# Two feed-forward layers in split float32: the second layer's first product by seven products of halves

## The chip, the cores and the metric

One core of one Trainium2 chip runs the program. Its engines are TensorE (PE in the rows), VectorE (DVE), ScalarE (ACT), GpSimd (POOL) and the DMA queues, which SyncE (SP) issues. The metric is the device time of one execution in microseconds. The profile is one execution taken by the hardware profiler.

## The reference

Linear attention with a normalised output, then two feed-forward layers. Only the second layer is changed.

```python
kv  = einsum('bhsd,bhse->bhde', k, v)                 # 4 batches, 8 heads, 576 tokens, 64
out = einsum('bhsd,bhde->bhse', q, kv)
x   = out / sqrt(mean(out*out) + 1e-6) * g_norm       # -> [2304 tokens, 512]
h = x @ w_in;  g = max(h, 0) + log1p(exp(-abs(h)));          x = g @ w_out      # first layer
h = x @ w_in2; g = where(h > 0, h, exp(min(h, 0)) - 1);    out = g @ w_out2     # second layer
```

The inner width d_ff is 2048. The weights are float64 in the reference; all results are float32.

## The kernel before

**Operands.** Every operand of the feed-forward products is carried as two parts, hi and lo, whose sum is the float32 value. A product a x b is three matmuls: hi x hi, lo x hi, hi x lo. The weights lie in DRAM as float64 words; `weights` turns a chunk of them into float32 by integer work (DMA L236, ACT L244 and L247, DVE L251, L255, L260 and L264) and splits it (ACT L271, DVE or POOL L275). A chunk has two halves: half 0 for the first product (w_in), half 1 for the second (w_out).

**Tiling.** The 2304 tokens go in 6 blocks of 384. d_ff goes in 16 chunks of 128, and these in 4 quarters. For each layer and quarter all blocks are swept; a block's sum over a quarter's 4 chunks stays in a PSUM bank and is added to `acc_sb` in SBUF at the quarter's end (L606 copies, L612 adds, L621 adds and L624 stores the result). A unit is (layer, quarter, block, chunk); each layer has 96. `unit_h` makes the first product of a unit (L486, 12 matmuls of 384 columns: 4 pieces of d_model x 3). `unit_act` applies the nonlinearity: in layer 1 seven instructions (L507 to L528), in layer 2 three (L507, L534, L537); then ACT casts the hi part (L541) and DVE or POOL makes the low part (L545). `unit_out` makes the second product three units later: in layer 1 four row chunks, in layer 2 three row chunks of 3 matmuls with 512 columns (L579 to L581). `next_x` (L630, L632) splits layer 1's sums into the token operands of layer 2.

**PSUM.** Two banks hold the h of two units, four the sums of the second product, one is used by transposes (`m`), one by attention (`o`).

**What sets the order.** The instructions are written as strands. The class `Order` (L47) lists them greedily: each engine's next instruction is the one with the lowest key among those it could start, by rough costs (`pe`, `act`, `dve`, `pool`, `dma`, L27 to L44), by marks that say what is there and by rings that count buffers. The order of each engine is then fixed in the program; each engine runs its list in turn and waits at an instruction until what it needs is there. `main` (L654) is PE's list of units; a strand of weights has the key of the unit that first needs them, less `W_LEAD`.

Of the kernel before, what the change touches and what calls it, by code (L numbers as in the profile page):

```python
# [25 lines left out]
# Rough costs in ns, for the order of issue alone.  # L26
def pe(n, passes=1):  # L27
    return passes * n / 2.4 + 3
# [18 lines left out]
class Order:  # L47
    """The order of issue: strands of instructions, listed greedily on the engines.

    A strand is a generator. Before each instruction it yields (engines, needs): a tuple of  # L50
    (engine, cost[, bias]) to choose from, and the marks that have to be there; it is sent the engine.
    Of the instructions that an engine could start, the one with the lowest key goes first. The
    data's own waits are the framework's; a poor estimate costs time only.
    """
# [9 lines left out]
    # From then on VectorE has the time, and GpSimd would only take its port from it.  # L64
# [9 lines left out]

    def add(self, key, strand):
        s = [key, strand, None, self.end if self.strands else 0.0]
        self.strands.append(s)
        s[2] = next(strand, None)
        if s[2] is None:
            self.strands.remove(s)  # L80
        return s

# [13 lines left out]
    def when(self, need):  # L96
        """The time a need is met, None if it isn't yet."""
# [20 lines left out]
    def run(self):  # L118
        while self.strands:
# [11 lines left out]
            if not heads:  # L131
                raise RuntimeError("no strand can go on")
# [13 lines left out]
            s[3] = self.end if e != PE else done  # L146
            try:
# [9 lines left out]
def linear_attention_then_two_ffns(  # L157
# [35 lines left out]
    WSLOTS = QF + 3  # L193
# [4 lines left out]
    ps = ctx.enter_context(tc.tile_pool(name="ps", bufs=1, space=bass.MemoryType.PSUM))  # L198

    # PSUM: its banks by use.  # L200
# [27 lines left out]
    w_t = {}  # L228
    convs = []

    def weights(i):
        layer, fc, half = convs[i]
# [8 lines left out]
        # The 29 bits that go, as a count of the last place that stays.  # L241
        yield ((ACT, act(512)),), [ring("r"), ("conv", i - 1)]
        r, r_h = sbuf("r", 1, f"r{n}", dtype=U32)
        nc.scalar.activation(r, low, AF.Copy, scale=2.0**-29)  # L244
        yield ((ACT, act(512)),), [ring("q")]
        q, q_h = sbuf("q", 3, f"q{n}", uses=2)
# [15 lines left out]
        # Below the smallest normal float32: zero.  # L262
# [3 lines left out]
        )  # L266
        drop(c_h)
        mark("conv", i)
        yield ((ACT, act(512)),), [ring(f"whi{half}"), ("split", i - 1)]
        hi, hi_h = sbuf(f"whi{half}", WSLOTS, f"whi{n}", dtype=F32R)  # L270
        nc.scalar.copy(hi, q)  # L271
        drop(q_h)
# [519 lines left out]
```

## Time and profile before

| | |
|---|---|
| time, median of 3 runs | 877.72 us (877.53 to 878.41) |
| span of the profiled execution | 875.8 us |
| PE busy | 860.6 us (98%) |
| DVE busy | 652.1 us (74%) |
| ACT busy | 490.2 us (56%) |
| POOL busy | 72.7 us (8%) |
| DMA, hardware queue | 52.44 MB, 18.3% of 16 engines |

The profiled execution is shown by its span, from the first to the last instruction; the times of the runs are taken around it. Layer 1's first product starts at 19.12 us, layer 2's at 462.13 us (its second unit at 467.92). Start and duration of an instruction come from the trace; matmuls are pipelined, so the distance from one start to the next says more of their cost than the duration of one.

### The profile page before, as it was taken

The numbers are of one execution on the slowest core, as the hardware profiler recorded it, in microseconds if no ns is written. First come the engines' busy times: TensorE is split into PE (matmuls) and PEld (weight loads), VectorE is DVE, ScalarE is ACT, GpSimd is POOL, SyncE is SP. The second block draws the span as 40 slices with busy tenths as digits, with TensorE's granted clock in tenths as the row PEclk, the third lists the DMA queues.
The fourth block names the chain that finished last, engine by engine and source line by source line (L and its number), as shares of the span: only waits on it lengthen the run. The fifth ranks groups of instructions, "written<-read, shape, count | busy, mean of one in ns | idle before, by whom it ended". The sixth has DMA issues, their size and how long they took to land.

```text
span 875.8 us, 12932 instructions
## 1 busy us (share of the span) xinstructions
PE 860.6 (98%) x4954; PEld 812.6 (93%) x4954; DVE 652.1 (74%) x1228; ACT 490.2 (56%) x1033; POOL 72.7 (8%) x62
## 2 busy tenths in 40 slices
PE   7999999999999999999999999999999999999998
PEld 7788899999999999999998999999999999999997
DVE  5899887788898887889999764787458864744543
ACT  4777887777676776667776544553234432322221
POOL 0441110010111000001021000000000000000000
PEclk8999999999999999999999999999999999999999
DMA  9953210201101101010011220122001200000111
GB/s 279 307 171 107 89 61 25 73 28 57 61 26 50 63 33 49 25 49 25 25 49 49 73 73 25 49 77 68 0 14 60 73 1 1 1 0 37 73 37 73
DMA packets 19519, 53.27 MB, mean 61 GB/s; under 512 B 2305, under 2 KB 5121, under 8 KB 19457
## 3 DMA queue, kind: packets, MB, share of 16 engines
q1 hardware_dynamic: 19456, 52.44, 18.3%
q8 instruction: 39, 0.64, 0.3%
q14 instruction: 24, 0.19, 0.1%
HBM read 47.71 MB, written 4.72 MB: 60 GB/s over the span
## 4 chain that ended last, share of the span: by engine, by line
PE 88%; DVE 8%; ACT 2%; issue 1%; DMA 1%; SPq 0%; DVEq 0%
PE h L486 42%; PE acc L580 14%; PE acc L581 14%; PE acc L579 14%; PE kv L313 1%; PE po L354 1%; DVE t L525 1%; DVE y L383 1%; DMA raw<-w 1%; DVE g L528 1%; DVE small L377 1%; DVE gl L545 1%; PE pt L399 1%; DVE g L522 1%; DVE c L255 0%
## 5 line engine op out<-in xcount | busy, mean ns | idle before, releaser
L486 PE MATMUL h<-xh,whi 128*128 128x384 f32 x768 | 259.3, 338 | 3.0 <-DVE g L522 3.0
L486 PE MATMUL h<-xh,wlo 128*128 128x384 f32 x768 | 258.9, 337 | 0.0
L507 ACT ACTIVATE e<-h 128x384 f32<-128x384 f32 x192 | 94.2, 491 | 197.0 <-PE h L486 194.4
L541 ACT CAST gh<-g 128x384 fp32r<-128x384 f32 x192 | 97.9, 510 | 138.2 <-DVE g L537 119.0
L486 PE MATMUL h<-xl,whi 128*128 128x384 f32 x768 | 164.5, 334 | 0.0
L545 DVE TENSOR_TENSOR gl<-g,gh 128x384 fp32r<-128x384 f32 x189 | 108.3, 574 | 64.4 <-ACT gh L541 63.1
L486 PEld LDWEIGHTS h<-xh,whi 128*128 128x128 f32 x768 | 144.2, 188 | 9.1 <-DVE g L522 3.8
L486 PEld LDWEIGHTS h<-xh,wlo 128*128 128x128 f32 x768 | 144.2, 188 | 4.0
L486 PEld LDWEIGHTS h<-xl,whi 128*128 128x128 f32 x768 | 136.0, 188 | 0.0
L579 PE MATMUL acc<-gh,whi 128*128 128x384 f32 x384 | 129.2, 336 | 0.0
L581 PE MATMUL acc<-gl,whi 128*128 128x384 f32 x384 | 128.4, 334 | 0.0
L580 PE MATMUL acc<-gh,wlo 128*128 128x384 f32 x384 | 128.3, 334 | 0.0
L581 PE MATMUL acc<-wlo,gh 128*128 128x512 f32 (+1 forms) x292 | 114.6, 393 | 0.0
L580 PE MATMUL acc<-whi,gl 128*128 128x512 f32 (+1 forms) x292 | 114.4, 392 | 0.0
L579 PE MATMUL acc<-whi,gh 128*128 128x512 f32 (+1 forms) x292 | 112.7, 386 | 0.0
L534 DVE TENSOR_SCALAR g<-e 128x384 f32<-128x384 f32 x96 | 37.4, 389 | 74.5 <-ACT e L507 74.2
L612 DVE TENSOR_TENSOR acc_sb<-acc_sb,acc 128x384 f32<-128x384 f32 (+1 forms) x108 | 62.5, 598 | 26.2 <-PE acc L581 25.9
L579 PEld LDWEIGHTS acc<-gh,whi 128*128 128x128 f32 x384 | 72.1, 188 | 0.1
L580 PEld LDWEIGHTS acc<-gh,wlo 128*128 128x128 f32 x384 | 72.1, 188 | 0.0
L581 PEld LDWEIGHTS acc<-gl,whi 128*128 128x128 f32 x384 | 72.0, 188 | 0.0
L260 POOL TENSOR_TENSOR c<-c,r 128x512 uint32<-128x512 uint32 x23 | 31.3, 1361 | 451.0 <-DVE c L255 433.9
L581 PEld LDWEIGHTS acc<-wlo,gh 128*128 128x128 f32 x292 | 54.8, 188 | 11.4
(120 smaller groups left out, 1099.9 us busy)
## 6 DMA issues: line engine op xcount, KB each, us to landing
raw<-w SPq DMA_DIRECT2D x64, 512.0 KB, 3.8
acc_sb<-kv SPq DMA_DIRECT2D x16, 512.0 KB, 6.2
out<-o SPq DMA_DIRECT2D x17, 256.0 KB, 2.1
q<-qt SPq DMA_DIRECT2D x15, 256.0 KB, 3.5
acc_sb<-kv_rest SPq DMA_DIRECT2D x16, 64.0 KB, 5.8
out<-o SPq DMA_DIRECT2D x2, 128.0 KB, 1.9
q('pair', 0)_106<-qt SPq DMA_DIRECT2D x1, 192.0 KB, 6.0
q('pair', 1)_121<-qt SPq DMA_DIRECT2D x1, 192.0 KB, 6.9
```

Source lines behind the costliest of these rows:

```text
L260: on(e).tensor_tensor(c, c, r, op=ALU.add)
L313: nc.tensor.matmul(p[i * D : (i + 1) * D, :D], t[:r, o + i * D : o + (i + 1) * D], t[:r, o + D2 + i * D : o + D2 + (i + 1) * D], start=(n ...
L354: nc.tensor.matmul(po[rows, cols], lhs(q), kvf[b % 2][:, c, :], start=True, stop=True)
L486: nc.tensor.matmul(ph, w[:, kc * P : (kc + 1) * P], xx[:, kc, :], start=(i == 0), stop=(i == len(products) - 1),)
L507: nc.scalar.activation(e, h, AF.Abs if layer == 0 else AF.Exp)
L534: nc.vector.tensor_scalar(g, e, 1.0, -1.0, op0=ALU.min, op1=ALU.add)
L541: nc.scalar.copy(gh, g)
L545: on(eng).tensor_sub(gl, g, f32(gh))
L579: nc.tensor.matmul(a, l[0], r[0], start=first, stop=False)
L580: nc.tensor.matmul(a, l[1], r[0], start=False, stop=False)
L581: nc.tensor.matmul(a, l[0], r[1], start=False, stop=last)
L612: nc.vector.tensor_add(a, a, p)
```

## The change

Layer 2's first product is computed by the scheme of Strassen in Winograd's form. Two token blocks and the two halves of d_model make a 2 x 2 matrix of token operands (a11, a12: the first block's halves; a21, a22: the second's), two chunks of d_ff and the same halves the matrix of weights. Seven products of halves replace eight; each is 6 matmuls of 384 columns (2 pieces of d_model x 3).

- **Slots.** A slot is (quarter, pair of blocks, pair of chunks), 24 in all in place of layer 2's 96 units. `slot_h` runs the products in the order 1, 6, 7, 5, 4, 2, 3. Products 1, 6, 7 and 4 add into one bank (A, tag `h`); after products 1, 6 and 7 the open sum is copied out by ACT (L778) or DVE (L780), as it is a part of more than one result. Products 5 and 3 add into bank B (tag `m`), product 2 into bank C (tag `o`). Three adds on DVE (L788: c22, c11, c12) bring bank and copy together. Between the products stand pieces of the second product, `some(n)`, three matmuls of 512 columns each (L914 to L916), taken from the pair of blocks before: slot 0 has the rest of layer 1, slot 1 has none, slots 2 to 23 have twelve each, 24 follow alone.
- **Activation.** `slot_act` works on 768 elements at a time: two chunks of d_ff of one block (L853 to L881).
- **Token operands.** `operands` makes seven per pair of blocks: sums on DVE (L691, L701), a cast on ACT (L705), a low part on DVE (L717), and a store of both parts to DRAM (L722, 768 KB). In quarters 1 to 3 they are read back (L712). Seven buffers hold them, so that the operand of the next pair takes the room of the same product's operand of the pair before, after its last use.
- **Weights.** `conv` and `split` are strands of their own; in layer 2 `split_pair` and `split_sums` make three sums of weight halves per pair of chunks and split them (L319 to L344). There are 6 buffers of each kind of split chunk for 7.
- **Order.** The cost `pe` is 0.4514 ns a column and 1 for 1/2.4 and 3; rings are merged (t and y into hk, g into hj, sq into e, gh and gl into G); the new keys are `X_LEAD`, `H_KEY` and `URGENT`.

```diff
 def pe(n, passes=1):
-    return passes * n / 2.4 + 3
+    return passes * n * 0.4514 + 1
...
-    WSLOTS = QF + 3
+    WSLOTS = QF + 2
+    NPAIR = NB // 2
+    FP = QF // 2
+    SLOTS = NQ * NPAIR * FP
+    OPS = (1, 6, 7, 5, 4, 2, 3)
...
+    def operands():
+        W = 2 * T
+        for p in range(NPAIR):
+            order.rekey(base(FP * NPAIR * 0 + FP * p) - X_LEAD)
+            top, low = acc_sb[2 * p], acc_sb[2 * p + 1]
+            a11, a12, a21, a22 = top[:, :W], top[:, W:], low[:, :W], low[:, W:]
...
+            nc.vector.tensor_add(s1, a21, a22)
+            of = {1: a11, 6: a11, 7: a21, 5: s1, 4: a22, 2: a12, 3: a12}
+            sums = {
+                6: [(a21, a11, a21, []), (a11, s1, a11, [("xop", 0, p, 1)])],
+                3: [(a12, a12, a11, [("xop", 0, p, 2)])],
+            }
+            for o in OPS:
+                for to, x, y, need in sums.get(o, []):
+                    yield ((DVE, dve(W)),), need
+                    nc.vector.tensor_sub(to, x, y)
+                yield ((ACT, act(W)),), [ring("sx")]
+                t = operand(0, p, o)
+                x = of[o].rearrange("p (k t) -> p k t", k=2)
+                nc.scalar.copy(t[:, :2, :], x)
+                order.add(order.now, low_part(p, o, t, x, s1_h))
+        for q in range(1, NQ):
+            for p in range(NPAIR):
...
+                for o in OPS:
+                    yield ((DMA, dma(P * 4 * T * 4)),), [ring("sx"), ("spilled", p, o)]
+                    nc.sync.dma_start(f32(operand(q, p, o)), spilled[p, o])
...
+    def slot_h(s, pieces):
...
+        yield from product(s, 1, lambda: open_("h", "A", 2), True, False, [ring("h")])
+        a, a_h = k["A"]
+        order.add(key - URGENT, copy("ca", "hj", 1, 0))
+        yield from some(2)
+        yield from product(s, 6, a, False, False, [("ca", s)])
+        order.add(key - URGENT, copy("cb", "hj", 6, 1))
+        yield from some(2)
+        yield from product(s, 7, a, False, False, [("cb", s)])
+        order.add(key - URGENT, copy("cc", "hk", 7, 1))
+        yield from some(1)
+        yield from product(s, 5, lambda: open_("m", "B"), True, False, [ring("m")])
...
+        order.add(key - URGENT, add_to("hk", 1, b, b_h, "c22", [("cc", s)]))
+        yield from some(2)
+        yield from product(s, 4, a, False, True, [("cc", s)])
+        order.add(key + H_KEY, slot_act(s, 1, k["hk"], k["A"]))
+        yield from some(1)
+        yield from product(s, 2, lambda: open_("o", "C"), True, True, [ring("o")])
...
+        yield from some(2)
+        yield from product(s, 3, b, False, True, [("c22", s)])
...
+        yield from some(99 if s == 0 else 2)
```

The diff changes the order of all engines. Two places show it, one on PE and one on DVE. The names of tiles: A, B and C are the banks, x0_1_6 is the token operand of quarter 0, pair 1, product 6, wx the sums of weights, G the split activations, whi1_2_1 the hi part of layer 2's chunk 2, half 1.

On PE, before, a unit of layer 2 is one run of 12 matmuls into one bank (the last 7 of them shown), then the second product of an earlier unit:

```order
L486 MATMUL h124_6508<-xh1_1_4743,wlo1_4_0_5625 128x384
L486 MATMUL h124_6508<-xh1_1_4743,whi1_4_0_5618 128x384
L486 MATMUL h124_6508<-xh1_1_4743,wlo1_4_0_5625 128x384
L486 MATMUL h124_6508<-xl1_1_4744,whi1_4_0_5618 128x384 x4
L579 MATMUL acc120_0_6483<-whi1_5_1_6226,gh121_6417 128x512
L580 MATMUL acc120_0_6483<-whi1_5_1_6226,gl121_6432 128x512
L581 MATMUL acc120_0_6483<-wlo1_5_1_6230,gh121_6417 128x512
L579 MATMUL acc120_1_6491<-whi1_5_1_6226,gh121_6417 128x512
L580 MATMUL acc120_1_6491<-whi1_5_1_6226,gl121_6432 128x512
L581 MATMUL acc120_1_6491<-wlo1_5_1_6230,gh121_6417 128x512
```

After, the third slot from its product 5 on; the second product's pieces stand between the products:

```order
L752 MATMUL B2_5561<-x0_1_5_5532,wx0_4737 128x384 [waits Activation_49]
L752 MATMUL B2_5561<-x0_1_5_5532,wx0_4737 128x384 x3
L752 MATMUL B2_5561<-x0_1_5_5532,wx0_4737 128x384 [waits DVE_49]
L752 MATMUL B2_5561<-x0_1_5_5532,wx0_4737 128x384
L914 MATMUL acc0_1_2_5534<-whi1_1_1_5379,G0_1_0_5443 128x512
L915 MATMUL acc0_1_2_5534<-whi1_1_1_5379,G0_1_1_5444 128x512
L916 MATMUL acc0_1_2_5534<-wlo1_1_1_5389,G0_1_0_5443 128x512
L914 MATMUL acc0_1_0_5508<-whi1_2_1_5592,G1_1_5571 128x512 [waits Activation_49]
L915 MATMUL acc0_1_0_5508<-whi1_2_1_5592,G1_1_5571 128x512 [waits DVE_49]
L916 MATMUL acc0_1_0_5508<-wlo1_2_1_5597,G1_1_5571 128x512 [waits DVE_49]
L752 MATMUL A2_5497<-x0_1_4_5539,whi1_1_0_4689 128x384
```

Products that added into one bank without a break are now apart, with a wait at the first matmul of a product, and the piece before product 4 waits for the cast and the low part of a weight chunk that ACT and DVE make.

On DVE, before, at the seam of the layers (units 93 and 94 of layer 1, its sums, and weights of layer 2):

```order
L632 TENSOR_TENSOR xl1_3_5122<-acc_sb3_71,xh1_3_5121 128x384
L275 TENSOR_TENSOR wlo1_1_1_5291<-q1_1_1_5192,whi1_1_1_5273 128x512 [waits Activation_49]
L522 SCALAR_TENSOR_TENSOR g93_5268<-h93_5224,g93_5268 128x384
L525 TENSOR_TENSOR t93_5289<-e93_5251,t93_5289 128x384 [waits Activation_49]
L612 TENSOR_TENSOR acc_sb4_72<-acc_sb4_72,acc88_0_5147 128x384 [waits PE_49]
L612 TENSOR_TENSOR acc_sb4_72<-acc_sb4_72,acc88_1_5154 128x384 [waits PE_49]
L612 TENSOR_TENSOR acc_sb4_72<-acc_sb4_72,acc88_2_5160 128x384 [waits PE_49]
L612 TENSOR_TENSOR acc_sb4_72<-acc_sb4_72,acc88_3_5166 128x384 [waits PE_49]
L528 TENSOR_TENSOR g93_5268<-g93_5268,t93_5289 128x384 [waits DVE_49]
L251 TENSOR_SCALAR c1_2_1_5337<-raw1_2_1_4908 128x512 [waits DMAHW3_49]
```

After, the rows that lead to that weight chunk's low part; the operands of the second pair of blocks (x0_1_3 is the last) stand ahead of it:

```order
L868 SCALAR_TENSOR_TENSOR hk1_5465<-hk1_5465,e1_1_5483 128x384
L701 TENSOR_TENSOR acc_sb2_72<-acc_sb2_72 128x768 [waits DVE_49]
L788 TENSOR_TENSOR hk2_5559<-hk2_5559,B2_5561 128x384 [waits PE_49,Activation_49]
L881 TENSOR_TENSOR G1_1_5571<-hk1_5465,G1_1_5571 128x768 [waits Activation_49]
L717 TENSOR_TENSOR x0_1_3_5577<-acc_sb2_72,x0_1_3_5577 128x768 [waits DMAHW2_49,Activation_49]
L860 TENSOR_SCALAR e1_0_5522<-e1_0_5522 128x768
L275 SCALAR_TENSOR_TENSOR c1_2_1_5485<-raw1_2_1_5088,c1_2_1_5485 128x512
L873 SCALAR_TENSOR_TENSOR hj1_5431<-hj1_5431,e1_0_5522 128x768 [waits DVE_49]
L280 ISA c1_2_1_5485<-c1_2_1_5485,r1_2_1_5391 128x1024 [waits DVE_49]
L284 SCALAR_TENSOR_TENSOR q1_2_1_5392<-q1_2_1_5392,c1_2_1_5485 128x512 [waits DVE_49]
L881 TENSOR_TENSOR G1_0_5587<-hj1_5431,G1_0_5587 128x768 [waits Activation_49]
L303 TENSOR_TENSOR wlo1_2_1_5597<-q1_2_1_5392,whi1_2_1_5592 128x512 [waits Activation_49]
```

What was spread over layer 1's last units (one `xl` of 384 at a time) is now a row of operands of 768 within the first slots of layer 2, in the same list as the slots' own sums and the weights.

On SP the seven re-reads of a pair's operands stand in one list with the weight loads; each re-read waits for PE (the last product that used the buffer), and the loads behind it are issued when it has been.

## Rows read from the trace of the kernel before

**Rows 1.** The page: span, and each engine's busy time, share and instructions.
```profile
span 875.8 us, 12932 instructions
...
PE 860.6 (98%) x4954; PEld 812.6 (93%) x4954; DVE 652.1 (74%) x1228; ACT 490.2 (56%) x1033; POOL 72.7 (8%) x62
```

**Rows 2.** Stretches: window and length, then each engine's busy time (x instructions), clock, DMA, GB/s.
```profile
40.00:80.00 40.00, 36.77 (x292) 33.71 (x291) 38.14 (x73) 31.00 (x73) 13.90 (x11) 1.00 0.55 175
320.00:360.00 40.00, 40.00 (x233) 40.00 (x232) 32.98 (x62) 26.43 (x57) 3.10 (x2) 1.00 0.08 27
440.00:480.00 40.00, 38.17 (x216) 37.27 (x215) 38.38 (x67) 28.55 (x60) 9.76 (x8) 1.00 0.13 43
520.00:560.00 40.00, 40.00 (x201) 36.12 (x200) 22.10 (x42) 18.51 (x35) 1.28 (x1) 1.00 0.13 40
560.00:600.00 40.00, 40.00 (x204) 36.42 (x203) 32.48 (x60) 20.81 (x40) 0.00 (x0) 1.00 0.23 72
```

**Rows 3.** Chain of waits over the seam of the layers: start us, us, what.
```profile
465.04 1.29 DVE xl L632
466.33 0.60 DVE wlo L275
466.93 0.47 DVE gl L545
467.40 0.48 DVE g L522
467.92 2.37 PE h L486 x12
```

**Rows 4.** Waits of PE up to 480 us: total, times, longest.
```profile
PE h L486 <- DVE g L522: 3.0, 5, 1.3
PE po('pair', 0)_116 L354 <- ACT kvf L326: 2.5, 1, 2.5
```

**Rows 5.** DVE's instructions by line and shape, 480 to 876 us.
```profile
L545 DVE TENSOR_TENSOR gl<-g,gh 128x384 fp32r<-128x384 f32 x93 | 51.9, 559 | 37.5 <-ACT gh L541 37.5
...
L534 DVE TENSOR_SCALAR g<-e 128x384 f32<-128x384 f32 x92 | 35.9, 391 | 74.4 <-ACT e L507 74.2
L612 DVE TENSOR_TENSOR acc_sb<-acc_sb,acc 128x512 f32<-128x512 f32 x36 | 24.7, 687 | 18.8 <-PE acc L581 18.6
...
L251 DVE TENSOR_SCALAR c<-raw 128x512 uint32<-128x512 uint32 x24 | 10.1, 419 | 0.0
```

**Rows 6.** Timeline in layer 2, from 564.8 us: start us, us, engine, line, operation.
```profile
566.37 0.39 PE L579 MATMUL acc<-whi,gh 128*128 128x512 f32 x1
...
566.60 0.40 PE L580 MATMUL acc<-whi,gl 128*128 128x512 f32 x1
...
566.63 0.49 ACT L507 ACTIVATE e<-h 128x384 f32<-128x384 f32 x1 [1.64 <-PE h L486]
```

**Rows 7.** Stretches of the start, columns as in group 2.
```profile
6.00:8.00 2.00, 0.18 (x2) 0.00 (x0) 0.28 (x2) 0.25 (x1) 0.00 (x0) 1.00 0.94 327
8.00:10.00 2.00, 1.30 (x6) 1.30 (x6) 1.56 (x3) 1.29 (x3) 0.00 (x0) 0.59 1.08 337
10.00:12.00 2.00, 2.00 (x23) 1.54 (x23) 1.09 (x3) 0.63 (x2) 0.00 (x0) 0.50 1.13 289
12.00:14.00 2.00, 2.00 (x10) 2.00 (x11) 0.48 (x4) 0.69 (x4) 0.00 (x0) 0.50 1.04 331
14.00:16.00 2.00, 2.00 (x26) 1.64 (x25) 1.19 (x3) 1.15 (x4) 0.64 (x1) 0.70 0.98 274
24.00:28.00 4.00, 4.00 (x56) 3.32 (x56) 3.93 (x8) 2.32 (x8) 0.39 (x1) 1.00 1.02 379
```

**Rows 8.** ACT's instructions by line and shape, 480 to 876 us.
```profile
L541 ACT CAST gh<-g 128x384 fp32r<-128x384 f32 x93 | 47.7, 513 | 114.5 <-DVE g L537 114.5
L507 ACT ACTIVATE e<-h 128x384 f32<-128x384 f32 x92 | 45.3, 492 | 125.0 <-PE h L486 123.7
```

**Rows 9.** The page: DMA issues, KB each, us to landing.
```profile
raw<-w SPq DMA_DIRECT2D x64, 512.0 KB, 3.8
```

More of the change, by code (lines that the diff above doesn't have):

```diff
@@ L228, in linear_attention_then_two_ffns, with conv @@
     w_t = {}
-    convs = []
-    def weights(i):
-        layer, fc, half = convs[i]
+    wx_t = {}
+    chunks = []
+    q_t = {}
+    def conv(i):
+        layer, fc, half = chunks[i]
         n = f"{layer}_{fc}_{half}"
@@ new lines, in unit_act @@
+        drop(e_h)
+        yield ((DVE, dve(T)),), []
+        nc.vector.scalar_tensor_tensor(g, h, 0.0, g, op0=ALU.max, op1=ALU.add)
+        drop(h_h)
+        eng = yield ((DVE, dve(T)), (POOL, pool(T), BIAS_T)), []
+        on(eng).tensor_sub(t, e, t)
+        drop(e_h)
+        yield ((DVE, dve(T)),), []
+        nc.vector.tensor_max(g, g, t)
+        drop(t_h)
+        yield ((ACT, act(T)),), [ring("G")]
+        G, G_h = sbuf("G", 4, f"G{n}", (P, 2, T), F32R)
+        nc.scalar.copy(G[:, 0, :], g)
@@ L585, in unit_out @@
+            nc.tensor.matmul(a, hi[:, c], gl, start=False, stop=last)
+            if k == KC - 1:
+                drop(G_h)
                 if j == NB - 1:
@@ L625, in unit_sum @@
             drop(o_h)
-    def next_x(j, i, a):
-        yield ((ACT, act(T)),), [("next_x", j, 0)] if i else [ring("xh"), ring("xl")]
-        xh, xl = x_tiles(1, j)
-        nc.scalar.copy(xh[:, i, :], a)
-        e = yield ((DVE, dve(T)), (POOL, pool(T), BIAS_X)), []
-        on(e).tensor_sub(xl[:, i, :], a, f32(xh)[:, i, :])
-        mark("next_x", j, i)
+    slots = [(q, p, q * FP + f) for q in range(NQ) for p in range(NPAIR) for f in range(FP)]
+    op_t = {}
+    spilled = {
+        (p, o): dr.tile([P, 4, T], F32, name=f"spill{p}_{o}", tag=f"spill{p}_{o}")
+        for p in range(NPAIR)
+        for o in OPS
+    }
@@ L662, in main, with rest, one @@
                 yield from unit_out(n - DELAY, acc)
+        def rest():
+            for n in range(NU - DELAY, NU):
+                left = unit_out(n, acc)
+                step = next(left, None)
+                while step is not None:
+                    box = [step]
+                    def one():
+                        e = yield box[0]
+                        try:
+                            box[0] = left.send(e)
+                        except StopIteration:
+                            box[0] = None
+                    yield one()
+                    step = box[0]
+        pieces = {0: rest()}
+        for s in range(SLOTS // FP):
+            q, p, _ = slots[FP * s]
+            for b in range(2):
+                last = s == SLOTS // FP - 1 and b == 0
+                pieces[FP * (s + 1) + 1 - b] = slot_out(q, p, b, last)
+        for s in range(SLOTS + 2):
+            entry[0] = base(s)
+            left = pieces.get(s, iter(()))
+            if s < SLOTS:
+                yield from slot_h(s, left)
+            for piece in left:
+                yield from piece
     def warm():
@@ L731, in linear_attention_then_two_ffns @@
         order.add(-18, setup())
-        for i, w in enumerate(convs):
-            k = keys[w]
-            order.add(CONV0 if i == 0 else k - W_LEAD, weights(i))
+        for i, w in enumerate(chunks):
+            k = CONV0 if i == 0 else need(*w) - W_LEAD
+            order.add(k, conv(i))
+            if w[0] == 0 or w[2]:
+                order.add(k, split(i, i))
+            elif w[1] % 2 == 0:
+                order.add(k, split_pair(i, i))
+        order.add(base(0), operands())
         for t in range(TT, NTT):
```

430 lines of the change are left out of this document (307 added, 123 removed).

## The prediction

> **What bounds the kernel now.** I read the page's table of busy shares first: in a span of 875.8 us PE is busy for 860.6, DVE for 652.1 and ACT for 490.2 [rows 1]. The reader is to see that only matrix work fills the span; DVE has a quarter free, but that is a mean. So the second view is the table by stretches [rows 2]. In the late part of layer 1 (320 to 360 us) PE is busy for all 40.00 us with 233 matmuls of 384 columns, 171.7 ns each, and DVE for 32.98. In layer 2 (520 to 600 us) PE is full again, with DVE at 22.10 and 32.48. In two stretches it is DVE that is full: 40 to 80 us (38.14, PE 36.77) and 440 to 480 us (38.38, PE 38.17), the seam between the layers. The third view, the chain of waits over that seam [rows 3], runs through DVE (L632, the low part of layer 2's tokens, then L522) until the second unit of layer 2 starts at 467.92; the table of waits gives the hole there, L486 waiting for DVE's L522, 1.3 us at its longest [rows 4]. So two things decide the forecast: in layer 2 each matmul removed shortens the span by itself, and at the seam each DVE instruction added may lengthen it.
>
> **What is removed.** Layer 2's first product is 96 units of 12 matmuls with 384 columns, 1152. The change makes 24 slots of 7 products of 6, 1008. 144 x 0.1717 = **-24.7 us**, all on the path as long as PE stays full.
>
> **What is added on DVE.** The longest form that the trace shows is 512 elements, the new ones have 768. Tensor-tensor work takes 559 ns for 384 and 687 for 512 [rows 5], 1.0 ns an element, so by this line 947 for 768; the bounds are 687 (no dearer than 512) and 1114 (twice the 384). Tensor-scalar work takes 391 and 419, so about 490 for 768. Per unit one wide instruction replaces two, which is cheaper; but the token sums and operands (three pairs x seven), the three adds that close the sums of each slot, and copies of the open sums come on top.
>
> What matters is where they stand. In the new order of DVE, from the add L788 that follows product 5 of the first slot to the low part wlo1_2_1 (L303) stand 45 instructions: 17 of 384, 16 of 768, 7 of 512 at 0.687, 4 tensor-scalar of 768 and one of 512: 9.5 + 15.1 + 4.8 + 2.0 + 0.4 = 31.7 us. Among them are all seven operands of the second pair of blocks and the conversion of a weight chunk. In the same stretch PE has 105 matmuls of 384 and 20 of 512, until L916 of the third slot asks for wlo1_2_1: 105 x 0.1717 + 20 x 0.231 (the start-to-start step [rows 6]) = 22.6 us. PE has nothing else to take, since its order is fixed and the second slot has no output pieces between its products. So PE must stand for 31.7 - 22.6 = 9.1 us, most of it in one hole at the L914 and L916 that name whi1_2_1 and wlo1_2_1, the rest in the second slot. Then there are DVE's own waits: six adds of the second and third slot (L788) stand in its order and wait for a product, about 0.5 us each by the 0.26 us from the next matmul's start to the reader's in rows 6 and as much again for where PE is in the product; 3 us. The next two marks leave PE no further behind: to the start of the fifth slot PE has 45.0 us and DVE, to that slot's first operand, 44.6. **+12 us**; with 768 at 687 ns and no such waits 4.9, with 1114 and 4 us of waits 15.8.
>
> **The clock after that hole.** At 6 to 8 us PE is nearly idle after a 2.5 us wait [rows 4], and in the following stretches the granted clock is 0.59, 0.50 and then 0.70 before it is whole again [rows 7]: about 6.5 us at 1.2 GHz instead of 2.4, 3.3 us lost. The hole of 1.3 us at the seam left it whole, 1.00 [rows 2]. The new hole is longer than the one at the start, but the work around it has DVE gaps of its own. **+2 us**, between 0 and 3.3. The Trainium skill's TensorE: Matmul & The Clock Gate ("What's actually happening") calls the halved clock the default which activity lifts; by that rule the loss would be the whole 3.3, and rows 7 agree with it for a hole at the start.
>
> **The copies out of open sums.** Products 1, 6, 7 and 4 add into one bank, which is copied out three times on the way; the next product into it waits for the copy. In between stand two pieces of the second product, 6 x 0.231 = 1.39 us. A copy needs 0.26 us before a reader starts [rows 6] and then 0.49 (L507 reads as much from a bank in 492 ns [rows 8]): with the hand-over back some 0.8 us. So a copy may start 0.6 us late for nothing. An instruction of 768 ahead of it on DVE (0.95) or on ACT (a cast of 384 takes 513 ns [rows 8], so at most 1.03) makes it later than that in 4 of 10 cases, by 0.2 us in the mean; 60 copies in the 20 slots that are left, with the engine busy in 8 of 10 cases, give 60 x 0.8 x 0.4 x 0.18 = 3.5 us; I take **+3**, as in some the copy stands with nothing ahead. Bounds: 0.5 (ACT takes all in time) and 20 (the rival below). The PSUM — Partial Sum Buffer page of the Trainium skill ("PSUM bank collisions raise a hardware error") says that no engine may read a bank while TensorE writes it, and that the order is for software to keep; so the wait can't be overlapped with matmuls into the same bank. No run here shows it, as the kernel before never reads an open bank.
>
> **Start and end of layer 1.** Layer 1's rows are kept, but its order is made anew with fewer weight buffers and merged rings. At 40 to 80 us DVE is the bound, and up to the 16th unit the new order has 2.4 to 2.9 us more DVE work, by the same durations: **+1.5** (-1 to 3). At the seam units 84 to 95 have 52.4 us of DVE rows for 48.9 before: **+1** of the 3.5 (0 to 4), as the first pair's operands are cut wide.
>
> **Costed at nothing.** The re-reads of the operands from DRAM, 63 of 768 KB, and 21 writes. 512 KB of weights land 3.8 us after issue [rows 9], so 5.7 by proportion; the buffer of an operand is free one slot (42 x 0.1717 + 36 x 0.231 = 15.5 us of PE work, less its own product) before its next use. The queues move 379 GB/s at 24 to 28 us [rows 7], at which 66 MB more are 174 us of a layer of 400. If that cover fails, a re-read that is a whole landing late stops PE for 5.7 us. Weight loads now stand behind re-reads that wait for PE on SP's queue, but the chunks behind them are used two slots later. POOL has 55 operations for 62.
>
> **The sum.** -24.7 + 12 + 2 + 3 + 1.5 + 1 = -5.2 us on the span of 875.8: 870.6. The median of the runs is 877.72, 1.9 above the profiled span, so **872.5 us**.
>
> **Rivals.**
> A, DVE keeps up: the 768-wide rows run at 687 ns and DVE enters layer 2 with a lead, so no hole and no clock loss. -24.7 + 3 + 1.5 + 1 = -19.2, **858.5 us**. For it: a third of DVE's time is free at 520 to 600 us [rows 2]. Against: rows 3 show DVE without a gap right up to layer 2, so there is no lead.
> B, the other side: the copies are late in every slot. Where two instructions stand ahead of a copy (0.95 + 0.56, less what is done of the first), it starts about 1.1 us late, 0.5 beyond the slack, for two of the three copies: 20 x 2 x 0.5 = 20 us in place of 3, **889.5 us**. It decides from a start 0.6 us late; at 0.8 us (40 x 0.2 = 8 us) the gain is gone. For it: DVE's order is fixed and has up to 15.6 us of rows, by the same durations, in slots of 15.5. Against: light slots have 9.2, and a copy may go to ACT, which has half its time free.
> C, the re-reads or the weights behind them are late: seven landings one after the other are 40 us for a pair of slots of 31, 9 us in each of 9 pairs: over 950. Against: the proportion that rows 7 show, 768 KB in some 2.1 us when several run at once.
> D, the change gives nothing: the hole at the seam is at its far end and the clock's loss too, the other three terms as above: -24.7 + 15.8 + 3.3 + 3 + 1.5 + 1 = -0.1, **877.6 us**. For it: if 768 elements cost twice 384, as no row excludes. Against: the two rows of rows 5 grow by 128 ns over 128 elements, so 559 holds some 175 ns that don't grow.
>
> **How the numbers follow.** This kernel can be told from no change beyond about 0.2%, 1.8 us, so same is 876.0 to 879.5. My forecast has 0.56, with a range of its own of 866 to 880; of it 0.43 lies in faster, 0.10 in same, 0.03 in slower. A has 0.12 (faster), B 0.13 (slower), C 0.05 (slower), D 0.10 (half same, half slower), and 0.04 is left for what I don't see (0.03 faster, 0.01 same). Faster 0.58, same 0.16, slower 0.26. The range leaves out the lower end of A, the upper half of B, and C: 860 to 888.
>
> **What would show it.** Right: 520 to 840 us with PE at 38 to 40 of 40 us, a hole of 7 to 9 us on PE between the second and the third slot, released by whi1_2_1 or wlo1_2_1 with DVE full before it, a dip of the granted clock behind it, waits of product 6 and 7 for their copies that sum to 2 to 5 us, and a 768-wide tensor-tensor near 0.95 us. Wrong: copies that PE waits for over 10 us in all (B), waits for x operands whose releaser is a DMA (C), no hole in the third slot (A), or a 768-wide row beyond 1.1 us.

## The result and the profile after

The changed kernel takes 862.10 us (median of four runs, 862.03 to 862.16) against 877.64 for the kernel before: a ratio of 0.9821, 95% interval 0.9809 to 0.9833. The forecast was 872.5 (860 to 888). So it is faster, as forecast, but by 15.5 us in place of 5.2.

The page of the changed kernel, the rows that answer to [rows 1]:

```profile
span 860.4 us, 12816 instructions
...
PE 839.6 (98%) x4814; PEld 788.4 (92%) x4814; DVE 695.5 (81%) x1266; ACT 509.1 (59%) x1027; POOL 59.7 (7%) x52
...
x<-spill SPq DMA_DIRECT2D x63, 768.0 KB, 5.4
```

PE still fills the span, with 21 us less work, and DVE has 43 us more. The re-reads land in 5.4 us, and PE waits for none of them.

Stretches of the changed kernel (columns as in [rows 2]):

```profile
460.00:480.00 20.00, 18.78 (x106) 17.95 (x106) 17.20 (x31) 11.94 (x23) 1.29 (x1) 1.00 0.16 52
480.00:500.00 20.00, 14.16 (x73) 12.70 (x72) 19.72 (x30) 10.76 (x17) 0.00 (x0) 0.94 0.71 275
500.00:520.00 20.00, 19.91 (x89) 17.63 (x89) 17.45 (x27) 12.58 (x22) 0.00 (x0) 0.89 0.42 149
520.00:660.00 140.00, 140.00 (x698) 125.79 (x697) 112.19 (x190) 70.41 (x122) 1.85 (x1) 1.00 0.66 232
660.00:680.00 20.00, 19.39 (x97) 17.14 (x96) 18.05 (x30) 10.80 (x20) 4.14 (x3) 1.00 0.52 185
```

The second row is the seam: PE 14.16 of 20 us, DVE 19.72. The clock is whole before it and 0.89 behind it. From 520 us PE is full for 140 us on end. The same columns, cut where the clock changes:

```profile
497.52:499.17 1.65, 0.00 (x1) 0.01 (x1) 1.61 (x3) 1.15 (x3) 0.00 (x0) 0.50 1.06 358
499.17:504.35 5.18, 5.18 (x14) 4.47 (x15) 4.05 (x7) 2.60 (x6) 0.00 (x0) 0.50 0.71 212
```

The clock falls to half (0.50, 1.2 GHz) while PE still stands in the hole; the matmuls of the next 5.18 us run at half, and from 504.35 us it is whole again.

PE's waits in the changed kernel (columns as in [rows 4]):

```profile
PE acc L914 <- ACT whi L299: 5.8, 1, 5.8
PE h L552 <- DVE g L586: 1.9, 2, 1.4
PE A L752 <- ACT hj L778: 1.8, 3, 0.6
...
PE A L752 <- DVE hj L780: 0.7, 1, 0.7
```

The first is the hole. The second lies in layer 1's first units, at 53 and 60 us. The other two are the copies: four late ones of 72, of which two stand in the second slot, which has no output pieces between its products. The chain of waits through the hole, which answers to [rows 3]:

```profile
493.37 0.95 DVE G L881
494.32 0.87 DVE x L717
495.19 0.47 DVE e L860
495.66 0.60 DVE c L275
496.26 0.87 DVE hj L873
497.13 0.61 DVE c L280
497.75 0.02 issue
497.77 0.70 DVE q L284
498.47 0.02 issue
498.50 0.63 ACT whi L299
499.12 0.04 issue
499.17 0.79 PE acc L914
```

PE's last matmul before the hole starts at 492.94. Each DVE row starts where the one before it ends or a little earlier; the chain cuts the overlap off, so 0.87 is what a row of 768 adds to a queue, 0.60 a row of 512, 0.47 one of 384 (a tensor-scalar of 768 takes about as much). The durations are longer. DVE's forms, 455 to 860 us, as in [rows 5]:

```profile
L860 DVE TENSOR_SCALAR e<-e 128x768 f32<-128x768 f32 x48 | 26.6, 555 | 24.6 <-ACT e L856 24.3
...
L873 DVE SCALAR_TENSOR_TENSOR hj<-hj,e 128x768 f32<-128x768 f32 x24 | 22.9, 953 | 0.3
```

**Where the 15.5 us are.** Layer 2's first matmul starts at 462.13 before and at 462.08 after, so nothing is lost or won ahead of it. From there to the span's end it is 413.7 before and 398.3 after, 15.4 less. After, PE stands for 1.2 us in the second slot, 5.8 in the hole and 1.3 in three other places (1.2 of it at two copies), 8.4 in all. The 5.18 us of matmuls at half the clock would take half as long at the whole: 2.6 us are lost. That leaves 387.3 us of PE at full clock against 412.3 (413.7 less the old hole of 1.3): the removal is worth 25.0. It is a remainder and also contains whatever else changed by a few tenths of a microsecond.

| term | forecast | measured |
|---|---|---|
| 144 matmuls fewer | -24.7 | -25.0 |
| PE stands at the seam (hole and second slot) | +12 | +7.1 |
| clock behind the hole | +2 | +2.6 |
| copies in the other slots | +3 | +1.3 |
| start and end of layer 1 | +2.5 | -0.1 |
| old hole of [rows 4] gone | not counted | -1.3 |
| sum, on the span | -5.2 | -15.4 |

### The profile page after: what moved, and what is told of

The parts are those of the page before. It is cut to its first block, busy times and chain, and to the rows that moved or that the text cites. A ratio compares the mean times of both kernels' runs of the same rounds, so it can differ in the third digit from the quotient of the medians.

```text
span 860.4 us, 12816 instructions
## 1 busy us (share of the span) xinstructions
PE 839.6 (98%) x4814; PEld 788.4 (92%) x4814; DVE 695.5 (81%) x1266; ACT 509.1 (59%) x1027; POOL 59.7 (7%) x52
## 4 chain that ended last, share of the span: by engine, by line
PE 87%; DVE 9%; ACT 1%; issue 1%; DMA 1%; SPq 0%; POOL 0%; DVEq 0%; POOLq 0%
PE h L552 21%; PE A L752 11%; PE acc L916 7%; PE acc L618 7%; PE acc L620 7%; PE acc L915 7%; PE acc L619 7%; PE acc L914 7%; PE B L752 5%; PE C L752 3%; PE kv L381 1%; PE po L428 1%; DMA acc_sb<-kv 1%; DVE g L592 1%; DVE y L457 1%
## 5 line engine op out<-in xcount | busy, mean ns | idle before, releaser
L552 PE MATMUL h<-xh,whi 128*128 128x384 f32 x384 | 130.2, 339 | 1.9 <-DVE g L586 1.9
L618 PE MATMUL acc<-G,whi 128*128 128x384 f32 x384 | 129.4, 337 | 0.0
L552 PE MATMUL h<-xh,wlo 128*128 128x384 f32 x384 | 128.4, 334 | 0.0
L620 PE MATMUL acc<-G,whi 128*128 128x384 f32 x384 | 128.4, 334 | 0.0
L619 PE MATMUL acc<-G,wlo 128*128 128x384 f32 x384 | 128.3, 334 | 0.0
L914 PE MATMUL acc<-whi,G 128*128 128x512 f32 (+1 forms) x292 | 113.3, 388 | 5.8 <-ACT whi L299 5.8
L916 PE MATMUL acc<-wlo,G 128*128 128x512 f32 (+1 forms) x292 | 115.4, 395 | 0.1
L915 PE MATMUL acc<-whi,G 128*128 128x512 f32 (+1 forms) x292 | 114.9, 393 | 0.0
L552 PE MATMUL h<-xl,whi 128*128 128x384 f32 x384 | 82.6, 334 | 0.0
L552 PEld LDWEIGHTS h<-xh,whi 128*128 128x128 f32 x384 | 72.1, 188 | 3.0 <-DVE g L586 2.4
L618 PEld LDWEIGHTS acc<-G,whi 128*128 128x128 f32 x384 | 72.1, 188 | 0.3
L620 PEld LDWEIGHTS acc<-G,whi 128*128 128x128 f32 x384 | 72.1, 188 | 0.0
L649 DVE TENSOR_TENSOR acc_sb<-acc_sb,acc 128x384 f32<-128x384 f32 (+1 forms) x108 | 62.3, 597 | 7.9 <-PE acc L620 7.2
L914 PEld LDWEIGHTS acc<-whi,G 128*128 128x128 f32 x292 | 55.1, 189 | 12.2 <-ACT whi L299 6.3
L916 PEld LDWEIGHTS acc<-wlo,G 128*128 128x128 f32 x292 | 55.0, 188 | 12.2 <-DVE wlo L303 0.8
L915 PEld LDWEIGHTS acc<-whi,G 128*128 128x128 f32 x292 | 55.1, 189 | 6.0
```

Of the source, the lines that this page charges most:

```text
L552: nc.tensor.matmul(ph, w[:, kc * P : (kc + 1) * P], xx[:, kc, :], start=(i == 0), stop=(i == len(products) - 1),)
L618: nc.tensor.matmul(a, hi[:, c], gh, start=first, stop=False)
L619: nc.tensor.matmul(a, lo[:, c], gh, start=False, stop=False)
L620: nc.tensor.matmul(a, hi[:, c], gl, start=False, stop=last)
L649: nc.vector.tensor_add(a, a, p)
L914: nc.tensor.matmul(a, gh, hi[:, w0:w1], start=(u == 0), stop=False)
```

## The experiments

All were timed against the kernel before in three rounds. PE's wait for the first queries differs from run to run (1.3 to 3.7 us), so where small differences matter I also give the stretch from layer 2's first matmul to the span's end: 398.3 for the changed kernel. It ran once more beside first, hoist_narrow and lead_late, without an edit:

> The new kernel itself, for the others to be set against on the same chip: 862.1 us within 0.8, if the differences of the runs come from the kernels and not from the chip.

862.16 us (862.03 to 862.86), with the same hole of 5.8.

### What the hole is made of

**due**: the second half's weights are due a slot earlier.

```
-            return base(fc // QF * FP * NPAIR + fc % QF // 2 + half * FP)
+            return base(fc // QF * FP * NPAIR + (FP if half else fc % QF // 2))
```

> The weight chunks that stopped the third slot (second half of chunks 2 and 3 of each quarter) get a due mark one slot earlier; nothing else is changed. In the order, wlo1_2_1 then stands 15 places further ahead on DVE, and the activation's low part that the same piece needs comes last. Theory 1, room on DVE: the hole is the surplus of DVE's rows over PE's work in the first slots, whatever stands last; the hole stays at 4 to 7 us with another releaser, 862 us within 2. Theory 2, the order: only this weight is late, and without it the next wait ends 4.8 us sooner; the hole falls to 1.5 us, the clock stays whole, 854 us.

864.7 (863.69 to 865.27). The weights are in time, but PE now waits for the second operand of the same matmuls:

```profile
PE acc L914 <- ACT G L879: 4.6, 1, 4.6
...
PE acc L915 <- DVE G L881: 0.9, 1, 0.9
```

5.5 us in place of 5.8, about as theory 1 had it. The time is above both expectations: two waits of 0.9 and 0.3 us for operands of the second pair come on top, the half clock falls on matmuls for longer, and layer 2 starts 1.1 us later. With the weights earlier, other rows that PE needs are late.

**fewdve**: the second pair's low parts are cast on ACT.

```
+        if p == 1:
+            yield ((ACT, act(2 * T)),), []
+            nc.scalar.copy(t[:, 2:, :], x)
...
```

> The low parts of the second pair's seven token operands are made as casts on ACT in place of subtractions on DVE (so the values are not the operand's low parts). DVE has 7 x 0.95 = 6.7 us less between the first slot and the hole. Theory 1: the hole of 5.8 us shrinks to under 0.5 us and the clock stays at its upper level, 862.1 - 5.8 - 3.0 = 853 us. Theory 2, or a chain of latencies: the weight is converted in its turn still; the hole shrinks by less than 3 us, 857 to 860 us.

860.04 (857.72 to 860.47), 393.9 from layer 2's first matmul: 4.4 less than the change. In place of the hole PE waits 1.4 us at this chunk and 1.2 at the next, and the clock at the seam is 1.00. ACT is busy for 17.03 of 20 us at 480 to 500: DVE has q ready at 491.7, and ACT comes to the cast only at 496.1. At this chunk the load went from one engine to the other.

**toact**: in the first four slots the step L860 runs on ACT as a Relu, and ACT alone makes the copies.

```
+        if s < 4:
+            yield ((ACT, act(2 * T)),), []
+            nc.scalar.activation(e, e, AF.Relu, scale=-1.0, bias=1.0)
+            plus = ALU.subtract
...
```

> In the first four slots the step min(e, 1) - 1 is made by ACT (as relu(1 - e), subtracted later) in place of DVE, and the copies out of the open sums go to ACT alone. In the stretch up to wlo1_2_1 DVE loses 4 tensor-scalar rows (0.49 us each by their starts) and 2 copies (0.55): 3.1 us; ACT, busy 10.8 of 20 us there, gets 4 x 0.84 + 2 x 0.48 = 4.3. Theory 1, room on DVE: the hole falls from 5.8 to 2.7 us, and as a wait of 2.6 us behind ACT's weight cast left the clock whole when the low parts were casts, the 3.0 us of the clock come back too: 856.5 us, within 1.5. Rival, a chain of latencies over ACT (cast of the weight, copies in turn): ACT becomes the releaser and the time stays at 860 to 863.

861.39 (860.62 to 862.04), a hole of 3.9 and 396.5 from layer 2's first matmul; the expected 856.5 was wrong. The edit took 3.1 us off DVE by its own count and 1.9 off the hole, so work taken off DVE does not come off the hole one for one.

**narrow** tests that: eleven DVE rows of the first two slots shrink to 32 columns, 6.3 us less, with every engine's order as in the changed kernel.

```
-                    nc.vector.tensor_sub(to, x, y)
+                    w = 32 if p == 1 else W
+                    nc.vector.tensor_sub(to[:, :w], x[:, :w], y[:, :w])
...
```

> The order of every engine is that of the new kernel; 11 DVE instructions in the first two slots are cut to 32 elements (3 sums of the second pair's tokens, the 4 tensor-scalar steps and 4 in-place adds of the activation), so those values are not computed in full. By the step from one start to the next that is 3 x 0.77 + 4 x 0.42 + 2 x 0.8 + 2 x 0.37 = 6.3 us less DVE work between the first slot's add and wlo1_2_1, and nothing is moved to another engine. Theory 1, room on DVE: the hole of 5.8 us falls to under 1 us and the clock stays whole: 862.1 - 5.8 - 3.0 = 853.5 us, within 1.5. Rival, latency through ACT's cast of the weight or the DMA: a hole of over 2.5 us stays, 857 us or more.

861.31 (860.74 to 861.81): the hole is 4.5, so 6.3 us of work bring 1.3. DVE's timeline shows why (start, us, engine, line; in brackets the idle time before and its releaser):

```profile
492.67 0.19 DVE L702 TENSOR_TENSOR acc_sb<-acc_sb 128x32 f32<-128x32 f32 x1
493.74 0.56 DVE L789 TENSOR_TENSOR hk<-hk,B 128x384 f32<-128x384 f32 x1 [0.88 <-PE B L753]
494.21 0.95 DVE L885 TENSOR_TENSOR G<-hk,G 128x768 fp32r<-128x768 f32 x1
```

The add L789 (L788 in the changed kernel) stands in DVE's order ahead of the chunk's conversion and needs a product of PE. I call such a place a tie. DVE now comes to it early and waits, 4.4 us over seven ties in the two slots. What was saved ahead of the last tie is lost there; the two rows saved behind it (0.4 and 0.8 us) are what the hole loses. From the add behind the first slot's product 5 to the start of wlo1_2_1 DVE idles for 5.9 us in all, where it idles for 1.4 in the changed kernel.

**first** puts the conversion of that chunk and its G ahead of four rows needed later (marks on L788, L701, the low part and L860).

```
+        late = [("w", 1, 2, 1)] if s == 2 else []
+        order.add(key - URGENT, add_to("hk", 1, b, b_h, "c22", [("cc", s), *late]))
...
```

> DVE's work is the same; by extra marks the five rows that convert the awaited weight chunk and the activation's low part for the same piece stand ahead of the rows that the third slot needs later (the operands of its products 2 and 3, the add behind product 5, the other half of the activation). Theory 1, room on DVE: the waits only move, to the operands of products 2 and 3 and to the next chunk: 5 to 7 us of waits in the third slot in all, 860 to 863 us. Theory 3, the rows between DVE's last wait for PE and the weight: the wait at wlo1_2_1 falls under 2 us, and the rows put off still come in time: 854 to 857 us.

864.05 (863.16 to 864.94):

```profile
PE acc L915 <- ACT whi L299: 6.9, 2, 5.5
```

1.4 us at that chunk, 5.5 at the next one's, 6.9 in all. The wait moved: this is theory 1's result (room on DVE), at 1 us more than its range, and theory 3's 854 to 857 is missed. Putting the chunk ahead of a tie is not enough when the rows put off are due right behind it.

**hoist_narrow** is narrow with the add behind the weight's low part.

```
+        late = [("w", 1, 2, 1), ("g", 1, 1)] if s == 2 else []
```

> The 11 DVE instructions cut to 32 elements as before (values not computed in full), and in the third slot the add behind product 5 put behind the weight's low part, so that DVE does not wait for that product on the way to the weight. Theory 3: the wait of 0.9 us and the add's 0.5 leave the path, the hole falls from 4.5 to about 3.2 us: 859.5 to 860.5. Theory 1: with 6.3 us less work and no wait DVE has all the room it needs; the hole falls under 1.5 us, the clock stays whole, 854 to 856 us.

861.55 (860.72 to 862.69), a hole of 4.7; both expectations missed. The tie is gone, and the next row takes its place, now by way of ACT:

```profile
492.71 0.17 DVE L863 TENSOR_SCALAR e<-e 128x32 f32<-128x32 f32 x1
493.56 0.96 DVE L886 TENSOR_TENSOR G<-hk,G 128x768 fp32r<-128x768 f32 x1 [0.67 <-ACT G L884]
```

That wait goes back through ACT's cast (L884, 492.69) to a row of DVE itself, L871, that ends just before. In the new order a second G, 0.87 us of DVE, also stands ahead of q, and a sum of the next operands ahead of wlo. So the run does not test the tie by itself, and no other does.

**lead5**: every weight chunk's conversion is planned five units ahead of its use in place of four.

```
-    W_LEAD = 4
+    W_LEAD = 5
```

> All weight strands get a key that is lower by one unit or slot quarter (W_LEAD 5 for 4), so their conversions stand earlier in the lists, those of chunks 2 and 3 ahead of the seam as far as buffers allow. If earlier weights take DVE rows out of the first slots into layer 1's last stretch, where DVE has 1 to 3 us in 20 left, the hole shrinks by 2 to 5 us: 855 to 860 us. If DVE is full there as well, the wait only moves (as with the earlier due mark): 862 us or more.

854.56 (853.81 to 855.16). No hole; 388.8 from layer 2's first matmul, 9.5 less, though DVE is busy for 19.67 and 20.00 of 20 us at 480 to 520. But layer 2 starts 2.1 us later: PE waits 4.0 us for y at the start of layer 1.

**lead_late** keeps the lead of four for what is due up to unit 32, so that the start is left alone.

```
-            k = CONV0 if i == 0 else need(*w) - W_LEAD
+            k = CONV0 if i == 0 else need(*w) - (5 if need(*w) > 32 else W_LEAD)
```

> W_LEAD 5 in place of 4 only for weights that are due after the 32nd unit; the kernel's start is as in the new kernel. With 5 for all, layer 2 took 388.9 us from its first matmul to the end of the span (398.3 in the new kernel), but the first matmul came 1.9 us later. Both gains together: 862.1 - 9.4 = 852.7 us, within 1. If the earlier start of layer 1's weights is a part of the gain: 855 or more.

**853.81 us (853.64 to 854.08), ratio 0.9728 [0.9713, 0.9742]**: right, and faster than both kernels. Its stretches:

```profile
480.00:500.00 20.00, 19.43 (x101) 17.53 (x100) 19.70 (x29) 12.99 (x22) 1.85 (x1) 1.00 0.67 269
500.00:520.00 20.00, 20.00 (x101) 17.97 (x101) 20.00 (x29) 13.80 (x23) 1.30 (x1) 1.00 0.61 229
```

DVE is at least as full as in the changed kernel, and PE stands only for its two copies in the second slot (1.1 us). whi1_2_1 is cast at 473.8 us in place of 498.5, ahead of the second pair's operands, and its low part, next, is one of those that the planner has put on POOL:

```profile
473.77 0.61 ACT L299 CAST whi<-q 128x512 fp32r<-128x512 f32 x1
474.46 1.30 POOL L303 TENSOR_TENSOR wlo<-q,whi 128x512 fp32r<-128x512 f32 x1 [8.49 <-ACT whi L299]
493.84 0.95 DVE L881 TENSOR_TENSOR G<-hk,G 128x768 fp32r<-128x768 f32 x1
```

The third row is now the last that this piece needs from DVE. From the add behind the first slot's product 5 (470.96) 33 rows stand ahead of it, 21.6 us, and DVE idles for 1.3; in the changed kernel 44 rows stand ahead of wlo1_2_1, 28.6 us, with 1.4 idle. PE's work in between is the same 22.6. So what makes the hole is not DVE's busy share, which is no smaller here, but the rows and waits of DVE that stand ahead of what PE needs next.

### The clock

**spin**: 24 matmuls whose result nobody reads stand on PE just ahead of the wait.

```
+            for _ in range(n):
+                nc.tensor.matmul(bank[:, :T], w, x, start=True, stop=True)
...
```

> 24 matmuls of 384 columns whose result nobody reads stand on PE ahead of the wait in the third slot (4.1 us of the 5.8 us hole); the order of all other engines is the same. If the idle hole is what brings the clock down to 0.94 and 0.89 in the two stretches behind it, the clock stays whole and the time falls by the 3.0 us that it cost, to 859 us. If the clock falls for another reason (the waits in the second slot), or if the extra matmuls delay what DVE waits for, 862 us or more.

861.3 (860.78 to 863.32). PE works for 4.4 us of the hole and idles for 1.65:

```profile
493.44 4.35 PE L801 MATMUL spin<-x,whi 128*128 128x384 f32 x24
499.43 0.50 PE L925 MATMUL acc<-whi,G 128*128 128x512 f32 x1 [1.65 <-ACT whi L299]
```

The clock of 480 to 520 is 1.00, and the way from layer 2's first matmul is 396.7: 1.6 us less, of the 2.6 that the half clock cost, and the median falls only by 0.8. The rest is a new wait: at full clock PE comes too early to the parts of this chunk and the next and stands again, 0.7 us over three places. One of them:

```profile
504.46 0.50 PE L925 MATMUL acc<-whi,G 128*128 128x512 f32 x1 [0.17 <-ACT whi L299]
```

lead_late, with neither hole nor half clock, runs the matmuls from this piece to product 3 of the slot 2.6 us faster than the changed kernel. By the Trainium skill (TensorE: Matmul & The Clock Gate, "What's actually happening") the halved clock is the default and activity lifts it; this pair of traces agrees: 5.8 us idle, 0.89 behind them; the same wait filled with work that serves nothing, 1.00.

**toact_spin** joins toact with 8 such matmuls.

> The same, with 8 matmuls of 384 that nobody reads (1.4 us) ahead of the wait in the third slot. By theory 1 the hole's rest is 1.3 us and the clock stays whole: 856.5 as without them, or up to 2 less if the clock fell without them. If they delay the work behind them: 857 to 858.

860.32 (859.45 to 862.13), a hole of 2.5 behind them, 394.9 from layer 2's first matmul, 1.6 less than toact. **lead5_spin** joins it with W_LEAD 5 and an operand lead (X_LEAD) of 4 in place of 3:

> The candidate for the best: W_LEAD 5, the relu step and the copies of the first four slots on ACT, operands asked for one unit earlier, and 8 matmuls ahead of the wait in the third slot. Theory 1 adds the parts up: 2 to 5 us from the earlier weights, 1.8 and 1.6 us measured for the other two from layer 2's start on: 853 to 857 us. If they all take the same hole, 858.

856.3 (855.36 to 857.24): in the range, but 1.7 us over lead5. With no hole there is nothing left for the 8 matmuls to save, and they are 8 x 0.17 = 1.4 us of PE's own time.

### The copies, the re-reads, the start

**nofill** puts all output pieces behind product 3, so that none stands between the products that share a bank (six lines like the first of these go).

```
-        yield from some(2)
...
-        yield from some(99 if s == 0 else 2)
+        yield from some(99 if s == 0 else 12)
```

> All pieces of the second product stand behind product 3 of a slot, none between the products, so nothing covers the copies out of the open sum. In the second slot, which has no pieces, a copy cost PE 0.57 and 0.65 us. My theory, that the pieces hide the copies: 2 waits of 0.6 us in each of 23 further slots, 28 us, 890 us. Rival, that PE's queue or the early end of a product hides them anyway: under 868 us. Rival, that each of the three copies and the adds are exposed: 3 x 0.8 x 23 = 55 us, 917 us.

892.72 (892.51 to 896.02), 1.0176 of the kernel before: right, and slower than it.

```profile
PE A L752 <- ACT hj L778: 26.6, 43, 1.6
PE A L752 <- DVE hj L780: 3.9, 5, 1.2
```

48 copies at 0.63 us. So the pieces between the products hide them: rival B's price is real, its condition was not met.

**twice** reads each operand from DRAM a second time into the same buffer.

```
+                    nc.sync.dma_start(f32(op_t[q, p, o][0]), spilled[p, o])
```

> Each re-read of an operand from DRAM is done twice, the second after the first has landed: 63 more transfers of 768 KB, 49.5 MB. If the re-reads are hidden behind a slot of matmuls, two landings of 5.4 us (10.8) still fit in 14.5: 862 us within 1. If they were at the edge (rival C), PE waits for x operands and each pair of slots grows by some us: over 870.

1044.77, 1.190 of the kernel before, and not 862:

```profile
PE B L753 <- DMA x<-spill: 56.0, 18, 5.1
PE C L753 <- DMA x<-spill: 30.6, 9, 4.3
PE A L753 <- DMA x<-spill: 25.3, 16, 2.7
```

112 us. The second read must wait for the first to land, and all later reads stand behind it on SP's queue, so an operand is complete only every 6.2 us. The rest of the 183 us is for the most part clock: 0.918 in the mean, where the changed kernel has 0.991. This is rival C's mechanism, and it measures the queue, not the traffic. **traffic** adds the bytes without the wait: behind each re-read a copy of as much from DRAM to a spare place in DRAM.

```
+                    nc.sync.dma_start(spare[p, o], spilled[p, o])
```

> Behind each re-read stands a copy of the same 768 KB from DRAM to DRAM that nothing waits for (63 more transfers); the order of all engines but SP is that of the new kernel. Reading twice one behind the other cost 182 us, with PE waiting for x operands. Theory A: that was the queue, in which each second read waited for the first to land, so that seven operands took seven landings; the transfers themselves have room, and here the time stays within 3 us of 862. Theory B: the 16 engines have no room for more bytes beside the re-reads (their share was up to 0.85); then landings grow from 5.4 to over 10 us and PE waits for operands: over 900 us.

884.16 (883.53 to 885.72), between the two expectations.

```profile
PE acc L921 <- DVE acc_sb L649: 8.7, 2, 4.9
...
PE B L759 <- DMA x<-spill: 3.4, 4, 2.1
...
x<-spill SPq DMA_DIRECT2D x63, 768.0 KB, 9.4
```

A landing grows from 5.4 to 9.4 us, and PE waits only 3.4 us for them. At 820 to 840 us the DMA share is 1.03 with 411 GB/s. So most re-reads can land 4 us later without a wait. The 8.7 us at L921 come from the weights behind them on the same queue. PE waits for DVE's L649, which stands in DVE's order behind the conversion of a weight chunk, and that waits for its load:

```profile
606.30 0.43 DVE L271 TENSOR_SCALAR c<-raw 128x512 uint32<-128x512 uint32 x1 [8.46 <-DMA raw<-w]
```

At 708.83 it waits another 8.69. These loads land 15 to 16 us after issue, where most in the changed kernel take 4 to 8. So in the changed kernel the weights, too, have cover, and twice the traffic uses it up: it costs 22 us.

**bcost** is the kernel before with one line of the change, the planner's new cost of a matmul.

```
-    return passes * n / 2.4 + 3
+    return passes * n * 0.4514 + 1
```

> The kernel before with only the planner's cost of a matmul changed to that of the new kernel (0.4514 ns a column and 1, for 1/2.4 and 3). My forecast put +2.5 us on layer 1's new order. In the profiles layer 1 ends within 0.1 us of where it did, though. If the new cost is what kept it so (a gain that covers 2.5 us of added work): 875 to 876 us. If the order of layer 1 costs and gains nothing: 877.7 within 0.8.

881.54, 1.0042 [1.0027, 1.0057] of the kernel before.

```profile
40.00:80.00 40.00, 34.62 (x271) 32.28 (x268) 37.99 (x77) 30.93 (x70) 13.36 (x10) 1.00 0.51 163
```

PE is at 34.62 of 40 us where it was at 36.77 [rows 2]. In the whole change it is at 36.41, so other edits take back what the new cost alone loses; which, I did not try. Layer 2 starts 5.7 us later (467.81), and from there to the end it takes 1.7 us less, as the old hole at its second unit is gone.

## Why the prediction was right and wrong

**The removal** was sized rightly from one row, 24.7 against 25.0.

**The seam** is the step that failed: 7.1 us where the sum had 12, half of the 10.2 us by which the span was missed. Place, releaser and cause are as forecast: the hole lies between the second and the third slot, at the L914 that names whi1_2_1, with DVE full before it. The hole itself is 5.8 us, where 7 to 9 was the sign of being right. Two terms of the sum were too large: the 45 DVE rows, which I summed by durations, and DVE's own waits, which I put at 3 us. In the trace after, DVE takes 30.0 us from the add behind product 5 of the first slot (469.25) to the start of wlo1_2_1 (499.25), 1.4 of it idle:

```profile
472.30 0.69 DVE L303 TENSOR_TENSOR wlo<-q,whi 128x512 fp32r<-128x512 f32 x1 [1.16 <-ACT whi L299]
483.96 0.55 DVE L788 TENSOR_TENSOR hj<-hj,C 128x384 f32<-128x384 f32 x1 [0.25 <-PE C L752]
```

So of the six adds that I let wait for PE one did, for 0.25 us; the other wait, for ACT, I had not seen. The 44 rows ahead of wlo1_2_1 take 28.6 us, where their durations sum to 31.1 (the terms of the forecast add up to 31.8 with wlo1_2_1, not 31.7). By the steps above they sum to 28.0: 17 x 0.47 + 16 x 0.87 + 6 x 0.60 + 4 x 0.50 + 0.45. With the trace's numbers the forecast's sum is 28.6 + 1.4 - 22.6 = 7.4. The steps could have been read before: the chain of [rows 3] shows 0.47 for a row that [rows 5] gives 559 ns. The duration of 768 itself was right, 947 forecast and 953 measured. The Trainium skill (VectorE: DVE Perf Modes, "The DRAIN you can't avoid") says that the next operation does not start until the pipe is empty, but one that is not held starts earlier; the trace agrees with the second half, by 0.08 us a row.

The sum also treats DVE's rows and DVE's waits as if they stood apart. narrow shows that they do not: rows saved ahead of a tie came back as waits. first shows that rows put behind come due at the next chunk, and lead_late that with 7.0 us fewer rows ahead the hole is gone. The last tie by itself was not tested.

**The clock** was 2.6 in place of 2, inside its bounds. That the hole makes the dip is shown by spin and lead_late, which have neither; of the time spin gave back 1.6, since PE then met other waits.

**The copies** cost 1.2 in place of 3 outside the second slot: nofill shows that the slack of the pieces covers them, as argued. Late ones are far rarer than the 4 in 10 I took: two of 69.

**Start and end of layer 1**: +2.5 forecast, nothing measured, the second largest part of the miss. I counted DVE's extra rows where DVE is full and let them stand; what PE lost there (0.36 of 40 us at 40 to 80) is less than what it won behind it (319.14 of 320 us at 120 to 440 before, 319.95 after). The measure is no finer than a microsecond: the same kernel's second profile (again) has layer 2's first matmul at 462.67.

**Not counted**: the old hole of 1.3 [rows 4] is gone. I had its row and credited nothing. The unit that waited is gone too, but in bcost that unit stands and the hole is gone as well, so a new order is enough.

**The re-reads at nothing**: right, no wait for any. That the time lies in the range of 860 to 888 is luck: the forecast's own range was 866 to 880, and the lower end was drawn for rival A. A's 858.5 lies nearest to the result, but by its mechanism (no hole) it is wrong: without the hole the kernel takes 853.8. Rivals B and C named true mechanisms whose conditions are not met, as nofill and twice show; D fell with the size of the 768 row.

## What to carry to other kernels

Sum a full engine's queue by start-to-start steps, not by durations. Where two engines' fixed orders are tied at several places, look for the last tie ahead of a wait: what is saved ahead of it can come back as a wait of the saving engine. Move the late operand's preparation to where the engine has room, well ahead (here a line of the planner, 8.3 us), and see that what it displaces is not due next. And credit the stalls that the removed work had of its own.

## What the runs showed of the hardware

- DVE's rows in sequence overlap by about 0.08 us: 953 ns of duration for 0.87 of step at 768 elements, 553 for 0.47 at 384.
- DVE rows are held up beside POOL. In the changed kernel 21 DVE rows took longer than the median of their line and shape by more than 0.15 us, and each of them ran beside a POOL operation; 97 others beside POOL kept their time. One tensor-tensor of 384 (L589 at 463.23 us) took 1.46 us, not 0.55, beside a POOL operation of 1.29 us (L280, from 462.99). No run was made to test it.
- PE's clock over 500 to 520 us was 0.92 behind a hole of 3.9 us (toact), 0.93 behind 4.5 (narrow), 0.89 behind 5.8 (the change) and 0.83 behind 5.5 (first). It was 1.00 behind holes of 2.5 (toact_spin), 1.65 (spin) and 1.4 and 1.2 (fewdve); spin and toact_spin have matmuls right ahead of theirs. The length alone does not decide it: in traffic the clock went to half behind a hole of 2.1 us that ended at 842.42 (columns as in [rows 2]):

```profile
843.37:846.78 3.41, 3.41 (x10) 2.84 (x10) 1.55 (x3) 0.84 (x1) 0.00 (x0) 0.50 0.19 70
```
